# An attention and mixture-of-experts kernel: the row of maxima leaves SyncE's queue for ScalarE's, and subtractions, transposes and gathers change their places in the order

## The chip, the cores and the metric

The kernel runs on one core of a Trainium2 chip. The metric is the device time of one execution in microseconds (us). Five engines work on their own instruction streams, each strictly in order: TensorE (PE, whose weight loads are listed as PEld), VectorE (DVE), ScalarE (ACT), GpSimd (POOL) and SyncE (SP), which here only issues transfers. An engine whose next instruction waits for a semaphore holds up everything behind it on that engine.

## The reference, cut to what matters

Four batches of eight heads, 576 positions, head size 64; then 2304 tokens of width 512 go to one of eight experts each (512 to 1024 to 512).

```python
q_rot, k_rot = rotate(q), rotate(k)                  # rotary embedding
scores = q_rot @ k_rot.T / sqrt(64)
scores -= max(scores, -1)
attn = exp(scores); attn /= attn.sum(-1) + 1e-9
x = (attn @ v) as [2304, 512]
logits = normalised(x) @ normalised(expert_emb).T / tau
expert_idx, gate_w = argmax(logits), its softmax weight
for e in range(8):
    out[mask_e] = gate_w * (relu(x[mask_e] @ w1[e]) @ w2[e])
```

## The kernel before

The work is cut into 16 pairs of heads (four pairs a batch) and then 22 slots of 128 tokens, each slot for one expert. Numbers are carried as a high and a low float16 part where precision needs it, so that many tiles exist twice (`qhi`, `qlo`, `khi`, `klo`, `xh`).

A pair's life: SP loads q and k (576 KB each); POOL rotates them (`rope` steps 0 to 2: two products and a sum for q, the same for k); ACT casts the high parts (step 3), POOL and DVE subtract to get the low parts (step 4: `qlo` on POOL, `klo` on DVE); SP copies them into the operand tiles `QAB`, `KA` and `KB` (`place`). TensorE then computes the scores once with queries as rows (`maxmm`), DVE reduces each block to its row maxima (`maxred`), and TensorE and ACT turn the ten columns of maxima into one row `mr` (`maxend`). That row is copied by a small DMA (2.5 KB, line 189) into row 64 of `QB`, the second half of `QAB`. The scores proper (`smm`, nine steps a pair) multiply `KA` by the queries (line 211) and add the product of `KB` with `QB` (line 215), whose 65th row subtracts the maxima; so line 215 of a pair can't start before its `mr` has landed. ACT takes the exponential (`sexp`, line 226), DVE splits some of it (`ssub`, line 235), TensorE multiplies by the values (`pvw`, `pv`) and DVE normalises into `X` (`pvend`, lines 279 to 283). `R.split` makes the two float16 parts of X: ACT casts the high part (line 450), POOL subtracts for the low part (line 452); every second pair SP transposes them for the router (`turn`) and writes them to memory (`write_x`).

The order on every engine is written by the program: each piece of work is put at a time on a planner's axis (nine units a pair; pair i starts its scores at 9 i), all are sorted by that time and emitted. The numbers of `TIMES` set these times. They are places in an order, not durations. PSUM for the two kinds of scores is a ring of three buffers shared by `maxmm` and `smm`.

After the attention come the slots. A slot gathers its tokens' rows by an indirect DMA that POOL issues (`gather`), SP transposes them by DMA (`xT`), TensorE runs the two layers (`ffn1`, `ffn2`), ACT and DVE split the hidden values, and POOL issues the scattering DMA of the result (`yout`). Each expert's weights come as eight pieces of 512 KB (`load`, into eight single buffers `raw`) where the slot's expert is a new one, and ACT and DVE split them in every slot (`conv`). The first four slots belong to the expert that is most frequent in the first three batches, so that they can start before the last batch is routed (`early`); the last batch's routing (`logits`, `finish`, `late`) runs beside them.

Of the kernel before, what the change touches and what calls it, by code (L numbers as in the profile page):

```python
# [7 lines left out]
F32 = mybir.dt.float32  # L8
F16 = mybir.dt.float16
# [8 lines left out]
B, H, S, D = 4, 8, 576, 64  # L18
NPAIR = 16
# [17 lines left out]
SY = SX * SW * SW  # L37

ORDER = ((0, 0, 0), (1, 0, 0), (0, 0, 1), (1, 0, 1), (0, 1, 0), (1, 1, 0))
TIMES = {"pe1": 1.06, "pvlead": 7.5, "mend": 10.5, "fin": 3, "w": 0.3, "pbufs": 13, "vat": -1, "med": 0.3, "sst": 1.6, "mct": 0.25, "pvt": 0.3, "pe0": 0.9, "d": 0.6, "rdt": 0.9, "e": 0.5, "c0": 126.4, "fin2": 5, "sq": 0.8, "max0": [[-21, 0.5], [0, 0.62], [6.2, 0.85]], "start": [-30, -13, -4, 2.6], "le": 105, "mmt": 0.2, "mlead": 14, "klo": 1, "me0": [-13.5, 6.6], "mdir": 1, "v0": 3, "pl": [[0, 0, 0, 3.3], [0, 1.0, 0.02, 0.1]], "setup": [-59.5, -25, -16.3, 0.7, -59.4, -12.5], "l3": -12, "rk": 23, "ls": 52, "dt": 0.6, "t0": 148.5, "ta": 0.25, "wlead": 10, "cut1": 126, "glead": 20, "s": 0.6, "fin3": -0.45, "r01": [[-30.0, -29.1, -28.2, -27.3, -24.6, -26.4, -25.5, -23.7, -22.8, -16.4], [-25, -24.9, -24.8, -15.5, -14, -24.7, -24.6, -24.5, -13.1, -13.0]], "bw": 2, "cp": [0, 2, 4, 6], "c0d": 4, "lg1": 0.5, "free": [[0.8, 1.4, 1], [2.0, 3.5, 1], [5.7, 6.2, 0]], "fgap": 1.2, "xd": [[0.3, 0.7, 2.8, 2.9], [0.3, 0.7, 2.0, 2.1]], "xd3": [0.02, 0.05, 0.3, 0.31], "xl": 13, "xg": 3, "xl0": 5, "lgd": [12, 12], "tail0": 15}  # L40


def attention(tc, ctx0, ctx, ctx2, ins, xs, R, at, bank, cfg):
    nc = tc.nc
# [14 lines left out]
    QAB, QA, KA, QB, KB = [], [], [], [], []  # L59
# [25 lines left out]
    st = {}  # L85
# [93 lines left out]
    def maxend(i, k):  # L179
        n = i % NB  # L180
        if k == 0:
            ps = bank("mt", 0)
            st["mt", i] = ps
            nc.tensor.transpose(ps[0:10, 0:128], st[i]["m9"], R.ident)
        else:
            ps = st.pop(("mt", i))
            mr = tp.tile([10, 128], F16, tag="mr", name=f"mr_{i}")
            nc.scalar.activation(out=mr, in_=ps[0:10, 0:128], func=AF.Identity, bias=shiftt[0:10], scale=-1.0)  # L188
            (nc.scalar if i == 0 else nc.sync).dma_start(out=QB[n][64:65, 0:1280], in_=mr)

    woven, late = [], []

# [100 lines left out]
    start = cfg["start"]  # L293
    O = cfg.get("o", {})
# [4 lines left out]
    for i in range(NPAIR):  # L299
        g0 = 9 * i  # L300
        r0 = start[i] if i < len(start) else g0 - L - RL
        rdt = cfg.get("rdt", .85)
# [10 lines left out]
        for k, (nm, step) in enumerate((("q", 0), ("q", 1), ("q", 2), ("q", 3), ("k", 0), ("k", 1), ("q", 4), ("k", 2), ("k", 3), ("k", 4))):  # L313
            y = r0 + (k + (step == 4 and nm == "k")) * rdt
            if i < 2:
                y = cfg["r01"][i][5 * (nm == "k") + step]
            if i == 2 and nm == "q" and step == 3:
                y = .2
            if i > 1:
                y += O.get(f"R{nm}{step}", 0)  # L320
            at(y, rope, i, nm, step)
            if step >= 3:
                z = y
                if i < 2:
                    z += cfg.get("pl", ((0, 0, 0, 0), (5, 5, 5, 5)))[i][2 * (nm == "k") + step - 3]
                else:
                    z += O.get(f"D{nm}{step}", 0)
                at(z, place, i, nm, ("hi", "lo")[step - 3])
            if step == 4 and i + 2 < NPAIR:
                at((y + .01 if nm == "q" else -13.06) if i < 1 else cfg.get("l3", -8) if i == 1 else max(-.9, y + .01), load, i + 2, nm)  # L330
# [3 lines left out]
        for s in range(9):  # L334
            ev(f"S{s}", g0 + s, smm, i, s)
            ev(f"E{s}", g0 + s + .1, sexp, i, s)
            ev(f"U{s}", g0 + s + cfg.get("sst", 1.05), ssub, i, s)
            mev(f"M{s}", m0 + md * s + cfg.get("mmt", .2), maxmm, i, s)
            mev(f"C{s}", m0 + md * s + cfg.get("mct", .25), maxred, i, s)
            ev(f"W{s}", g0 + PVL + s + cfg.get("pvt", .3) - .81, pvw, i, s)  # L340
            ev(f"P{s}", g0 + PVL + s + cfg.get("pvt", .3), pv, i, s)
            if s in (4, 8):
                ev(f"X{s // 5}", g0 + PVL + s + cfg.get("pe0", 1.04), pvend, i, s // 5, 0)
                ev(f"Y{s // 5}", g0 + PVL + s + cfg.get("pe1", 1.06), pvend, i, s // 5, 1)
                y = g0 + PVL + s + cfg.get("pe1", 1.06)
                d = cfg["xd"][s // 5] if i < NPAIR - 1 else cfg["xd3"]
                for k in range(2):
                    at(y + d[k], R.split, i, s // 5, k)
                if i % 2:
                    at(y + d[2], R.turn, i, s // 5)  # L350
                    at(y + d[3], R.write_x, i, s // 5)
# [8 lines left out]
class Routing:  # L360
# [93 lines left out]
    def turn(self, i, g):  # L454
        b, kb = i // 4, i % 4 // 2
        if g == 0:
            self.XT[b, kb] = self.xp.tile([128, 9, 2, 128], F16, tag="xt", name=f"xt_{b}_{kb}", bufs=3)
        c = slice(0, 5) if g == 0 else slice(5, 9)
        self.nc.sync.dma_start_transpose(out=self.XT[b, kb][:, c].rearrange("p s t c -> p (s t) c"), in_=self.XH[b, kb][:, c].rearrange("p s t c -> p (s t c)"))

# [237 lines left out]
def moe(tc, ctx, ins, out, xs, R, raw, cfg):  # L698
# [4 lines left out]
    P = {}  # L703

    def open1():
        P["w1"] = pool(name="wring1", bufs=5, side="right")

    def open2():
        P["m"] = pool(name="mtmp", bufs=2, side="right")
# [102 lines left out]
def build(tc, ins, out, cfg=None):  # L812
    cfg = {**TIMES, **(cfg or {})}
    nc = tc.nc
    with ExitStack() as ctx:
# [15 lines left out]
        if True:  # L831
# [40 lines left out]
            for b in range(B):  # L872
# [152 lines left out]
```

## Time and profile before

| | us |
|---|---|
| median of three runs | 632.31 (632.26 to 640.57) |
| the profiled execution | 629.74 |
| its span, first to last instruction | 628.0 |
| TensorE busy | 517.4 (82%) |
| VectorE busy | 473.7 (75%) |
| ScalarE busy | 344.6 (55%) |
| GpSimd busy | 273.0 (43%) |

The shares are means over stages with different limits: the start to about 66 us, eleven pairs to about 259 us, the last pairs with the first routing work to about 358 us, the passage to the experts to about 405 us, and the experts' slots to the end. The profile's page also lists who waited for whom, and where the kernel's time went is read from there stage by stage.

### The profile page before, as it was taken

The page shows a single profiled execution, that of the slowest core. Times are in us where ns is not written, and L with a number is a line of the kernel's source. Part 1 is how long each engine was busy: PE and PEld are TensorE (multiplying, and loading weights), DVE is VectorE, ACT ScalarE, POOL GpSimd, SP SyncE. Part 2 cuts the span into 40 slices and gives each one's busy share as a digit, 9 for nine tenths or more (in the row PEclk, how much of TensorE's full clock was granted, in tenths as well). Part 3 has the DMA queues.
Part 4 walks back from the last instruction along what each step waited for, and adds up shares of the span by engine and source line. Part 5 has one row for each costly group of instructions (what it writes and reads, how often), then busy time and mean ns, then how long its engine had stood idle before and what let it go on. Part 6 is the DMA issues. An engine that isn't in the chain of part 4 may idle for free. (4 is left out here: it accounts for less than half of the span.)

```text
span 628.0 us, 15414 instructions
## 1 busy us (share of the span) xinstructions
PE 517.4 (82%) x5894; PEld 411.2 (65%) x5894; DVE 473.7 (75%) x708; ACT 344.6 (55%) x556; POOL 273.0 (43%) x207
## 2 busy tenths in 40 slices
PE   2488877967897789777688769999899999799994
PEld 1157766856776668666577767868577776586761
DVE  5678877668776775898668516569899999879981
ACT  2244444543433643443445633269789897779862
POOL 6995585648566855774112504213122221411201
PEclk9999789877977896897979978999999999889997
DMA  7875557376295473651762262168934569943210
GB/s 234 227 197 165 154 113 178 92 185 180 69 181 154 104 180 102 149 131 32 176 250 60 60 116 55 44 173 263 300 79 100 152 190 331 294 134 85 70 35 26
DMA packets 87809, 91.35 MB, mean 145 GB/s; under 512 B 50726, under 2 KB 72614, under 8 KB 87728
## 3 DMA queue, kind: packets, MB, share of 16 engines
q1 hardware_dynamic: 83708, 79.27, 49.0%
q0 software_dynamic: 3520, 10.58, 5.7%
q8 instruction: 48, 0.79, 0.5%
q10 hardware_dynamic: 500, 0.45, 0.3%
q14 instruction: 33, 0.27, 0.1%
HBM read 110.60 MB, written 10.56 MB: 193 GB/s over the span
## 5 line engine op out<-in xcount | busy, mean ns | idle before, releaser
L735 DVE SCALAR_TENSOR_TENSOR w<-raw,w 128x1024 f16<-128x1024 f32 x148 | 173.4, 1221 | 18.4 <-ACT w L734 18.4
L226 ACT ACTIVATE p<-st 128x576 f32<-128x576 f32 x144 | 92.3, 646 | 127.3 <-PE st L215 127.1
L175 DVE TENSOR_REDUCE m<-mx 128x1 f32<-128x576 f32 x144 | 107.2, 752 | 66.8 <-PE mx L167 64.8
L245 PEld LDWEIGHTS pv<-V,p 128*128 128x128 f32 (+1 forms) x800 | 118.4, 204 | 54.6 <-issue 51.4
L734 ACT ACTIVATE w<-raw 128x1024 f16<-128x1024 f32 x148 | 146.6, 1047 | 8.2 <-DMA raw<-w 8.2
L761 PE MATMUL h<-xTm,w 128*128 128x128 f16 x2112 | 127.4, 224 | 13.7 <-DMA xTm<-xg 12.9
L761 PEld LDWEIGHTS <-w 128*128 128x128 f16 x2112 | 124.8, 100 | 19.2 <-issue 7.6
L245 PE MATMUL pv<-V,p 128*128 128x65 f32 (+1 forms) x800 | 122.4, 268 | 1.2 <-ACT mr L188 1.2
L215 PE MATMUL st<-QAB,KB 65*128 65x288 f16 x320 | 86.1, 320 | 41.5 <-DMA QAB<-mr 41.5
L782 PE MATMUL yp<-w,hT 128*128 128x512 f16 x528 | 117.5, 379 | 0.0
L787 POOL DMA_INDIRECT out<-y,sidx x22 | 29.1, 1321 | 178.0 <-ACT y L786 168.5
L211 PE MATMUL st<-QAB,KA 128*128 128x288 f16 x320 | 93.3, 313 | 6.0 <-DVE m L175 3.7
L782 PEld LDWEIGHTS <-hT 128*128 128x128 f16 x528 | 50.8, 98 | 57.4 <-issue 0.2
L452 POOL TENSOR_TENSOR xh<-x,xh 128x320 f16<-128x320 f32 (+1 forms) x30 | 26.9, 896 | 121.5 <-ACT xh L450 113.4
L167 PE MATMUL mx<-KA,QAB 128*128 128x288 f16 x300 | 68.6, 325 | 13.3 <-DVE m L175 5.6
L235 DVE TENSOR_TENSOR p<-p 128x576 f16<-128x576 f32 x64 | 70.0, 1093 | 0.7 <-ACT p L226 0.7
L268 PE MATMUL pv<-V,p 128*128 128x65 f16 (+1 forms) x400 | 53.8, 200 | 0.6 <-DVE p L235 0.6
L266 PE MATMUL pv<-V,p 128*128 128x65 f16 (+1 forms) x400 | 54.3, 203 | 0.0
L267 PE MATMUL pv<-V,p 128*128 128x64 f16 (+1 forms) x400 | 54.2, 203 | 0.0
L772 DVE SCALAR_TENSOR_TENSOR hT<-h,hT 128x512 f16<-128x512 f32 x44 | 30.2, 686 | 26.8 <-ACT hT L767 26.8
L167 PEld LDWEIGHTS <-QAB 128*128 128x128 f16 x300 | 32.6, 110 | 25.1 <-issue 15.3
L215 PEld LDWEIGHTS <-KB 65*128 65x128 f16 x320 | 43.8, 145 | 6.5 <-POOL k L122 2.8
(159 smaller groups left out, 676.4 us busy)
## 6 DMA issues: line engine op xcount, KB each, us to landing
raw<-w SPq DMA_DIRECT2D x152, 512.0 KB
q<-qk SPq DMA_DIRECT2D x16, 576.0 KB
k<-qk SPq DMA_DIRECT2D x16, 576.0 KB
v<-v SPq DMA_DIRECT2D x16, 320.0 KB
QAB<-qhi SPq DMA_DIRECT2D x32, 144.0 KB
KA<-khi SPq DMA_DIRECT2D x58, 72.0 KB
xs<-xh SPq DMA_DIRECT2D x16, 256.0 KB
QAB<-qlo SPq DMA_DIRECT2D x32, 72.0 KB
```

What stands on the lines that cost most here:

```text
L167: nc.tensor.matmul(ps[:, c, :288], lhsT=QA[n][:, cols(s, h)], rhs=KA[n][:, H0[h] + c * 288:H0[h] + c * 288 + 288], start=(h == hs[0]), sto ...
L175: nc.vector.tensor_reduce(out=m[:, c:c + 1], in_=st.pop(("mx", i, s))[:, :, :288], op=ALU.max, axis=AX.XY)
L211: nc.tensor.matmul(ps[:, c, :288], lhsT=KA[n][:, cols(s, h)], rhs=QA[n][:, H0[h] + c * 288:H0[h] + c * 288 + 288], start=(h == hs[0]), sto ...
L215: nc.tensor.matmul(ps[:, c, :288], lhsT=KB[n][0:65, cols(s, h)], rhs=QB[n][0:65, H0[h] + c * 288:H0[h] + c * 288 + 288], start=False, stop ...
L226: nc.scalar.activation(out=p.rearrange("p (c x) -> p c x", c=2), in_=st.pop(("s", i, s))[:, :, :288], func=AF.Exp, scale=0.125)
L235: nc.vector.tensor_tensor(out=lo, in0=p, in1=hi, op=ALU.subtract)
L245: nc.tensor.matmul(o, lhsT=lt, rhs=rt, start=first, stop=False, skip_group_check=True)
L266: nc.tensor.matmul(o[:, 0:65], lhsT=ph, rhs=vv[:, 0:65], start=False, stop=False, skip_group_check=True)
L734: nc.scalar.activation(out=d[:, 0], in_=raw[c], func=AF.Copy, scale=SW)
L735: nc.vector.scalar_tensor_tensor(out=d[:, 1], in0=raw[c], scalar=SW, in1=d[:, 0], op0=ALU.mult, op1=ALU.subtract)
L761: nc.tensor.matmul(ps[:, f], lhsT=wd[:, wi, jj * 512 + f * 128:jj * 512 + f * 128 + 128], rhs=xt[:, 4 * jj + 2 * jp + xi], start=(jp == 0 ...
L782: nc.tensor.matmul(ps, lhsT=ht[:, hi, 2 * c + ii], rhs=wd[:, wi, ii * 512:(ii + 1) * 512], start=(c == 0 and k == 0), stop=(c == 3 and k = ...
```

## The change

Four things change; the amount of work does not. First, the small DMA of `mr` is issued by ACT for every pair (before: for pair 0 alone, SP for the rest). Second, for pairs 0 to 10 POOL's subtraction of the first half of X stands behind the rotations that it stood in the middle of, and SP's transposes and writes of X move behind the placing of the next k parts; SP also issues a pair's `qlo` behind the next load of q. Third, the gathered rows and their transposes get a pool of their own that opens at an earlier switch (`open1`), so that the gathers of the first four slots stand earlier on POOL, and SP's transposes of every slot stand further ahead in SP's queue (`xl` 13 to 20; `glead` moves too). Fourth, the router's transposed X has two buffers in place of three, and the last batch's logits stand later on TensorE (`tail0` 15 to 18).

```diff
-TIMES = {... "glead": 20, ... "xd": [[0.3, 0.7, 2.8, 2.9], [0.3, 0.7, 2.0, 2.1]], ... "xl": 13, ... "xl0": 5, ... "tail0": 15}
+TIMES = {... "glead": 30, ... "xd": [[0.4, 3.9, 5.9, 5.91], [0.3, 0.9, 3.0, 3.01]], "xd2": [0.2, 0.5, 2.0, 2.01], "xi": 11, "pd": [0.3, 1.2, 0.3, 0.3], ... "gx": 12, "xl": 20, ... "xl0": 10, ... "tail0": 18}
...
-            (nc.scalar if i == 0 else nc.sync).dma_start(out=QB[n][64:65, 0:1280], in_=mr)
+            nc.scalar.dma_start(out=QB[n][64:65, 0:1280], in_=mr)
...
-                    z += O.get(f"D{nm}{step}", 0)
+                    z += cfg["pd"][2 * (nm == "k") + step - 3]
...
-                d = cfg["xd"][s // 5] if i < NPAIR - 1 else cfg["xd3"]
+                d = cfg["xd"][s // 5] if i < cfg["xi"] else cfg["xd2"] if i < NPAIR - 1 else cfg["xd3"]
...
-            self.XT[b, kb] = self.xp.tile([128, 9, 2, 128], F16, tag="xt", name=f"xt_{b}_{kb}", bufs=3)
+            self.XT[b, kb] = self.xp.tile([128, 9, 2, 128], F16, tag="xt", name=f"xt_{b}_{kb}", bufs=2)
...
     def open1():
         P["w1"] = pool(name="wring1", bufs=5, side="right")
+        P["x"] = pool(name="xgath", bufs=4, side="right")
...
-        xg = P["m"].tile([128, PITCH], F32, tag="xg", name=f"xg_{t}", bufs=4)
+        xg = P["x"].tile([128, PITCH], F32, tag="xg", name=f"xg_{t}")
...
-        d = st["xT", t] = P["m"].tile([128, 8, 128], F16, tag="xT", name=f"xTm_{t}", bufs=3)
+        d = st["xT", t] = P["x"].tile([128, 8, 128], F16, tag="xT", name=f"xTm_{t}", bufs=3)
...
                     e1 = plan(t, gen, "c" * 5 + ".b" + "d" * 4)
+                    end11 = end
...
-                sc.at(max(T0 + DT * (G - cfg.get("glead", 22)), ready) if t >= NE else max(cut2 + .05, e1) + t * .01, M["gather"], t)
+                sc.at(max(T0 + DT * (G - cfg.get("glead", 22)), ready) if t >= NE else max(end11 + cfg["gx"], e1) + t * .01, M["gather"], t)
```

ACT's stream in a pair of the steady part, after the change (`p` are the exponentials of the steps, `mr` the row of maxima of the next pair, `khi` and `xh` casts):

```order
L226 ACTIVATE p_5_678<-st_5_671 128x576
L188 ACTIVATE mr_700<-mt_688,shiftt 10x128
L189 DMA QAB_135<-mr_700 1x10x128
L226 ACTIVATE p_6_710<-st_6_703 128x576
L226 ACTIVATE p_7_737<-st_7_729 128x576
L125 CAST khi_742<-k_421 128x576
```

The DMA of line 189 is the row that is new on ACT; before, these rows stood there without it and the row stood on SP, as the next piece shows.

SP's queue in such a pair before (`QAB<-qhi`, `QAB<-qlo`, `KA<-khi`, `KB<-klo` place the parts of a later pair; `q` and `k` are loads of 576 KB):

```order
L139 DMA QAB_135<-qhi_1122 64x2x576 x2
L141 DMA QAB_135<-qlo_1219 64x576 x2
L90 DMA q_1223<-qk 128x1152
L189 DMA QAB_129<-mr_1237 1x10x128
L144 DMA KA_136<-khi_1277 64x576
```

and after:

```order
L139 DMA QAB_135<-qhi_1122 64x2x576 x2
L90 DMA q_1220<-qk 128x1152
L141 DMA QAB_135<-qlo_1218 64x576 x2
L144 DMA KA_136<-khi_1276 64x576
L145 DMA KA_136<-khi_1276 64x576
```

The row of maxima no longer stands behind the placing of `qlo`, which POOL's subtraction has to release.

POOL's stream in such a pair before (line 452 makes the low part of X, lines 118 to 122 rotate, line 130 subtracts for `qlo`):

```order
L118 TENSOR_TENSOR k_423<-k_423,cost 128x576
L452 TENSOR_TENSOR xh_0_636<-x_620,xh_0_636 128x5x64
L120 TENSOR_TENSOR k_423<-k_423,sint 128x576
L130 TENSOR_TENSOR qlo_685<-q_346,qhi_583 128x576
L122 TENSOR_TENSOR k_423<-k_423 128x576
L452 TENSOR_TENSOR xh_0_636<-x_620,xh_0_636 128x4x64
```

and after:

```order
L118 TENSOR_TENSOR k_421<-k_421,cost 128x576
L120 TENSOR_TENSOR k_421<-k_421,sint 128x576
L130 TENSOR_TENSOR qlo_684<-q_344,qhi_581 128x576
L122 TENSOR_TENSOR k_421<-k_421 128x576
L452 TENSOR_TENSOR xh_0_636<-x_620,xh_0_636 128x5x64
L452 TENSOR_TENSOR xh_0_636<-x_620,xh_0_636 128x4x64
```

Both subtractions of X now follow the last sum of the rotations. On POOL at the passage to the experts, after the change (`w_2`, `w_4` are parts of weights; `xg` the first gathers; `xh_1` belongs to pair 14):

```order
L733 TENSOR_TENSOR w_2_4530<-ws_4531,w_2_4530 128x1024
L745 DMA xg_4653<-xs,gidx 128x520
L745 DMA xg_4655<-xs,gidx 128x520
L745 DMA xg_4657<-xs,gidx 128x520
L745 DMA xg_4659<-xs,gidx 128x520
L452 TENSOR_TENSOR xh_1_4668<-x_4053,xh_1_4668 128x5x64
L452 TENSOR_TENSOR xh_1_4668<-x_4053,xh_1_4668 128x4x64
```

Before, the two subtractions of pair 14 stood ahead of the four gathers.

## Rows read from the trace of the kernel before

**Rows 1.** Waits view: waiting group, releaser, us in total, times, longest.

```profile
PE st L215 <- DMA QAB<-mr: 41.5, 13, 5.0
```

**Rows 2.** Timeline of PE: start, us, instruction, idle time before it and its releaser.

```profile
68.02 0.40 PE L215 MATMUL st<-QAB,KB 65*128 65x288 f16 x1 [1.90 <-DMA QAB<-mr]
...
89.20 0.40 PE L215 MATMUL st<-QAB,KB 65*128 65x288 f16 x1 [4.09 <-DMA QAB<-mr]
...
109.80 0.40 PE L215 MATMUL st<-QAB,KB 65*128 65x288 f16 x1 [3.85 <-DMA QAB<-mr]
...
259.02 0.38 PE L215 MATMUL st<-QAB,KB 65*128 65x288 f16 x1 [3.95 <-DMA QAB<-mr]
```

**Rows 3.** Timelines of ACT, POOL and SP, 99 to 107 us.

```profile
100.85 0.34 ACT L188 ACTIVATE mr<-mt,shiftt 10x128 f16<-10x128 f32 x1
...
99.44 0.79 POOL L452 TENSOR_TENSOR xh<-x,xh 128x320 f16<-128x320 f32 x1 [6.05 <-ACT xh L450]
...
102.11 1.83 POOL L130 TENSOR_TENSOR qlo<-q,qhi 128x576 f16<-128x576 f32 x1
...
103.97 1.13 SPq L141 DMA_DIRECT2D QAB<-qlo  x2
...
105.83 0.81 SPq L189 DMA_DIRECT2D QAB<-mr  x1
```

**Rows 4.** Windows: us, busy of PE, PEld, DVE, ACT, POOL, clock, DMA share, GB/s.

```profile
85.10:89.20 4.10, 0.01 (x2) 0.00 (x1) 3.64 (x5) 1.64 (x5) 3.65 (x3) 0.90 0.95 210
89.20:95.30 6.10, 6.10 (x39) 4.71 (x39) 2.38 (x4) 1.85 (x4) 4.12 (x3) 0.51 0.72 183
95.30:105.90 10.60, 10.60 (x150) 9.72 (x150) 8.59 (x15) 5.07 (x10) 5.87 (x4) 1.00 0.78 152
...
48.10:66.10 18.00, 15.71 (x197) 13.70 (x196) 16.34 (x25) 8.60 (x16) 9.23 (x7) 1.00 0.56 163
```

**Rows 5.** Windows by stage.

```profile
66.10:259.00 192.90, 154.97 (x1755) 134.15 (x1754) 141.83 (x216) 85.01 (x182) 124.94 (x85) 0.82 0.58 140
...
358.00:405.00 47.00, 37.69 (x507) 31.73 (x508) 19.47 (x62) 16.65 (x37) 10.33 (x8) 0.89 0.40 82
405.00:628.00 223.00, 206.14 (x2270) 148.50 (x2266) 189.74 (x186) 172.49 (x202) 48.34 (x38) 0.97 0.57 158
```

**Rows 6.** Timelines of ACT and PE at pair 0.

```profile
20.04 1.52 ACTq L189 DMA_DIRECT2D QAB<-mr  x1
...
22.47 0.64 PE L215 MATMUL st<-QAB,KB 65*128 65x288 f16 x2 [2.37 <-DMA QAB<-mr]
```

**Rows 7.** Lines 235 and 122 by source: count, ns min/median/max, first and last start.

```profile
L235 DVE TENSOR_TENSOR p<-p x64: 794/1052/2010, 38.8 to 355.0; 128x576 f16<-128x576 f32 x64
...
L122 POOL TENSOR_TENSOR k<-k x15: 1391/1400/1949, 19.7 to 297.4; 128x576 f32<-128x576 f32 x15
```

**Rows 8.** Timelines of POOL, SP and PE at the passage to the experts.

```profile
345.62 2.14 POOL L732 TENSOR_TENSOR w<-ws,w 128x1024 f16<-128x1024 f32 x1 [2.64 <-ACT w L731]
...
355.22 1.58 POOL L744 DMA_INDIRECT xg<-xs,gidx  x1 [0.29 <-issue]
...
359.32 1.23 SPq L749 DMA_TRANSPOSE xTm<-xg  x1
...
364.11 2.74 PE L761 MATMUL h<-xTm,w 128*128 128x128 f16 x24 [6.18 <-DMA xTm<-xg]
```

**Rows 9.** Timeline of PE: the last batch's logits.

```profile
377.75 0.18 PE L489 MATMUL lg<-emb,xt 128*128 128x16 f16 x1 [3.20 <-DMA xt<-xh]
```

**Rows 10.** Timelines of PE and ACT in the experts' slots.

```profile
447.40 5.52 PE L761 MATMUL h<-xTm,w 128*128 128x128 f16 x96 [2.55 <-DMA xTm<-xg]
...
547.52 7.93 PE L761 MATMUL h<-xTm,w 128*128 128x128 f16 x96 [4.14 <-DMA xTm<-xg]
...
549.04 1.06 ACT L734 ACTIVATE w<-raw 128x1024 f16<-128x1024 f32 x1 [2.90 <-DMA raw<-w]
```

**Rows 11.** Timeline of SP: the placing of the low part of k.

```profile
93.20 1.10 SPq L147 DMA_DIRECT2D KB<-klo  x2
```

More of the change, by code (lines that the diff above doesn't have):

```diff
@@ L39 @@
 ORDER = ((0, 0, 0), (1, 0, 0), (0, 0, 1), (1, 0, 1), (0, 1, 0), (1, 1, 0))
-TIMES = {"pe1": 1.06, "pvlead": 7.5, "mend": 10.5, "fin": 3, "w": 0.3, "pbufs": 13, "vat": -1, "med": 0.3, "sst": 1.6, "mct": 0.25, "pvt": 0.3, "pe0": 0.9, "d": 0.6, "rdt": 0.9, "e": 0.5, "c0": 126.4, "fin2": 5, "sq": 0.8, "max0": [[-21, 0.5], [0, 0.62], [6.2, 0.85]], "start": [-30, -13, -4, 2.6], "le": 105, "mmt": 0.2, "mlead": 14, "klo": 1, "me0": [-13.5, 6.6], "mdir": 1, "v0": 3, "pl": [[0, 0, 0, 3.3], [0, 1.0, 0.02, 0.1]], "setup": [-59.5, -25, -16.3, 0.7, -59.4, -12.5], "l3": -12, "rk": 23, "ls": 52, "dt": 0.6, "t0": 148.5, "ta": 0.25, "wlead": 10, "cut1": 126, "glead": 20, "s": 0.6, "fin3": -0.45, "r01": [[-30.0, -29.1, -28.2, -27.3, -24.6, -26.4, -25.5, -23.7, -22.8, -16.4], [-25, -24.9, -24.8, -15.5, -14, -24.7, -24.6, -24.5, -13.1, -13.0]], "bw": 2, "cp": [0, 2, 4, 6], "c0d": 4, "lg1": 0.5, "free": [[0.8, 1.4, 1], [2.0, 3.5, 1], [5.7, 6.2, 0]], "fgap": 1.2, "xd": [[0.3, 0.7, 2.8, 2.9], [0.3, 0.7, 2.0, 2.1]], "xd3": [0.02, 0.05, 0.3, 0.31], "xl": 13, "xg": 3, "xl0": 5, "lgd": [12, 12], "tail0": 15}
+TIMES = {"pe1": 1.06, "pvlead": 7.5, "mend": 10.5, "fin": 3, "w": 0.3, "pbufs": 13, "vat": -1, "med": 0.3, "sst": 1.6, "mct": 0.25, "pvt": 0.3, "pe0": 0.9, "d": 0.6, "rdt": 0.9, "e": 0.5, "c0": 126.4, "fin2": 5, "sq": 0.8, "max0": [[-21, 0.5], [0, 0.62], [6.2, 0.85]], "start": [-30, -13, -4, 2.6], "le": 105, "mmt": 0.2, "mlead": 14, "klo": 1, "me0": [-13.5, 6.6], "mdir": 1, "v0": 3, "pl": [[0, 0, 0, 3.3], [0, 1.0, 0.02, 0.1]], "setup": [-59.5, -25, -16.3, 0.7, -59.4, -12.5], "l3": -12, "rk": 23, "ls": 52, "dt": 0.6, "t0": 148.5, "ta": 0.25, "wlead": 10, "cut1": 126, "glead": 30, "s": 0.6, "fin3": -0.45, "r01": [[-30.0, -29.1, -28.2, -27.3, -24.6, -26.4, -25.5, -23.7, -22.8, -16.4], [-25, -24.9, -24.8, -15.5, -14, -24.7, -24.6, -24.5, -13.1, -13.0]], "bw": 2, "cp": [0, 2, 4, 6], "c0d": 4, "lg1": 0.5, "free": [[0.8, 1.4, 1], [2.0, 3.5, 1], [5.7, 6.2, 0]], "fgap": 1.2, "xd": [[0.4, 3.9, 5.9, 5.91], [0.3, 0.9, 3.0, 3.01]], "xd2": [0.2, 0.5, 2.0, 2.01], "xi": 11, "pd": [0.3, 1.2, 0.3, 0.3], "xd3": [0.02, 0.05, 0.3, 0.31], "gx": 12, "xl": 20, "xg": 3, "xl0": 10, "lgd": [12, 12], "tail0": 18}
 def attention(tc, ctx0, ctx, ctx2, ins, xs, R, at, bank, cfg):
```

## The prediction

> **What bounds the kernel now.** I read the waits view first, for TensorE, since it is busy most. Its largest wait is that of line 215 for the DMA of `mr`: 41.5 us in 13 waits [rows 1]. The timeline places them: one at the first step of each pair from pair 2 to pair 11, ten in all, the first before 68.02 us, the last before 259.02 us, most of them close to 4 us [rows 2]; the others are the 2.37 us of pair 0 and small ones near the end, which I leave out.
>
> Why `mr` comes late is read from ACT, POOL and SP beside each other [rows 3]. ACT has the row ready at 100.85 + 0.34 = 101.19. SP issues its DMA only at 105.83, because `qlo` stands ahead of it in SP's queue and waits for POOL's subtraction, which runs from 102.11 to 103.94. POOL is late because its subtraction of X waited 6.05 us for ACT's cast and holds the rotations behind it. From issue to TensorE's start is 109.80 - 105.83 = 3.97 us. So of the 8.6 us between the row and its use, 4.64 pass before anything is sent.
>
> What a pair costs without the wait: the stretch around the wait before 89.20 shows TensorE idle for 4.10 us, then busy without a gap for 6.10 us at a granted clock of 0.51 and for 10.60 us at 1.00 [rows 4]. 0.51 is the lower of its two levels, 1.2 GHz, and it comes right behind the idle 4 us. At 2.4 GHz the 6.10 us would be about 3.1, and TensorE's own work in a pair 13.7. VectorE did 3.64 us of its work in the idle stretch, so it has 3.64 + 2.38 + 8.59 = 14.6 us in this pair, and 141.83 / 9 = 15.8 on the mean of the nine pairs [rows 4, 5]. VectorE is therefore next.
>
> **The change part by part.** *The row of maxima on ACT.* It removes the wait for `qlo` from the path. ACT's own DMA of pair 0 took from 20.04 to 22.47, 2.43 us, until TensorE started [rows 6]; SP's took 3.97. From 101.19 that lands at 103.6 or at 105.2; line 215 wants it at 109.80 - 3.85 = 105.95. Both are in time, so I take the wait as gone. The issue occupies ACT for 0.8 us (SP's row) to 1.5 us (ACT's own) a pair; ACT is busy 85.01 of 192.90 us [rows 3, 5, 6] and waits mostly for TensorE's scores, so I price it at nothing; without that cover it is 9 x 1.5 = 14 us.
>
> *What is late next.* With the wait gone a pair can't be shorter than VectorE's 15.8 us. A pair that had no such wait and ran at a granted clock of 1.00 is in the trace: pair 1, where VectorE was busy 16.34 of 18.00 us and idle 1.66 [rows 4] (more reductions fall there than in a later pair). 15.8 of work and 1.0 to 1.7 of idle time make 16.8 to 17.5; the gapless part of a pair with half its clock lost is 6.10 + 10.60 = 16.7. I take 17.0. The stretch from 66.10 to 259.00 holds the first wait and nine pairs, 192.9 us [rows 5]; nine pairs of 17.0 are 153, a gain of 40. Bounds: 15.8 a pair (VectorE never idle) gives 192.9 - 142 = 51; 18.3, worked out below as a rival, gives 28.
>
> *POOL's subtractions behind the rotations.* `qlo`, `khi` and the loads of q and k come earlier by the 6 us that POOL waited; they are two to three pairs ahead of their use, so this earns nothing itself, but it keeps POOL off the path: POOL's 124.94 / 9 = 13.9 us a pair [rows 5] fit in 17.0 as one block. The low part of X and its transposes come later by some units; the router reads them more than a pair later in batches 0 and 1, which hides it. If that cover were gone, one transpose's landing, some 5 us (359.32 to 364.11 [rows 8]), would show twice. SP's new order (`qlo` behind a load, transposes behind `klo`) costs nothing for the same lead. The transposed X with two buffers: by the planned times the logits that read the older tile stand ahead of the transpose that overwrites it, so nothing waits.
>
> *The last pairs.* From 259 to 358 us only one short wait for `mr` is left, and routing work on VectorE and a late transpose hold TensorE; none of that is touched. I take 1 us, between 0 and 4.
>
> *The first gathers.* They were issued from 355.22 on, behind the subtractions of pair 14; now they follow the weights' subtraction that ends at 345.62 + 2.14 = 347.76 [rows 8]. Gather to transpose took 359.32 - 355.22 = 4.1 us and transpose to TensorE 364.11 - 359.32 = 4.8, so the rows land at about 347.8 + 8.9 = 356.7, and TensorE, idle from 364.11 - 6.18 = 357.9, finds them. That returns 6.18 us. The 24 matmuls behind the wait took 2.74 us; the same 24 by the pace of the slots, 5.52 for 96 [rows 10], take 1.4, so another 1.3 us come back, of which with the following matmuls I take 1.5. The logits of the last batch now stand behind one more such block of 24, which fills 1.3 of the 3.20 us that they wait [rows 9]. Sum 9; bounds 3 (the gathers wait for the lists and half is lost) and 11 (both waits whole). The cost, pair 14's subtractions some 2 to 3 us later, falls on tiles that are transposed with pair 15.
>
> *Transposes further ahead.* In SP's queue a slot's transpose now stands ahead of four weight loads. The two large waits of the slots are for such transposes: 2.55 and 4.14 us, and the second is followed by 96 matmuls in 7.93 us in place of 5.52 [rows 10], 9.1 in all. The loads that it overtakes come later, and ACT already waits 2.90 us for one beside the second wait [rows 10]. I take 6 of 9.1; bounds 0 and 9.1. The other slots have no gap to close.
>
> **The sum.** 40 + 1 + 9 + 6 = 56 us. From the profiled execution's 629.74 that is 573.7; it lies 2.6 below the median of 632.31, so I add 2.6: 576. The bounds of the terms together are 28 + 0 + 3 + 0 = 31 and 51 + 4 + 11 + 9 = 75: 601 and 557.
>
> **The rivals.** *GpSimd and VectorE in each other's way.* The same subtraction of line 235 takes 794 to 2010 ns and the same sum on POOL 1391 to 1949 [rows 7]: the two slow each other when they meet, and in shorter pairs they meet more often. If they excluded each other, POOL's 13.9 us and VectorE's four subtractions at 0.79 with some 1.2 us for its other two of the kind would make 18.3 us a pair. That is a gain of 28 in place of 40: 588. For it: POOL now works in one block; against it: part of POOL's 13.9 is already such waiting. The Trainium skill, "SBUF — State Buffer", section "Who interferes with whom", says that a VectorE operation with two inputs in SBUF and a GpSimd operation that reads SBUF exclude each other, the later one waiting in full; the spread of both rows agrees with it. Chance 0.16.
>
> *The row still lands late.* More transfers are in flight beside it, and if it took twice SP's price, 7.9 us, it would land at 109.1 and 3.2 us of each wait would stay: 9 x 3.2 = 29 less, 605. Against it: most of its delay was before the issue. The Trainium skill, "DMA: Bandwidth & Descriptors", section "Issuing engines are not separate DMA queues", says that another issuing engine only saves the sequencer's time, the transfers sharing the same 16 DMA engines; taken alone that would leave a gain of SP's 0.81 us a pair, and no row here shows more than the queue's part of it. Chance 0.06.
>
> *VectorE was the bound all along.* The 3.64 us that it works in the idle stretch would be paid elsewhere, and a pair would shrink by only 4.10 - 3.64 = 0.5: 4 + 16 = 20 in all, 612, or no measurable change if the later terms fail too. Against it: in the rest of the pair VectorE is idle 16.70 - 10.97 = 5.7 us [rows 4]. Chance 0.09.
>
> *Slower: ACT held by its own DMA.* By its semaphores, ACT's DMA waits for the transfer eight places earlier, in every second pair the placing of `klo`, which SP issues. Everything behind it on ACT, the exponentials above all, waits too. Now `klo` goes out at 93.20 [rows 11], 8.0 us before the row is ready at 101.19, and if it lands 4 us later, as the row does now, the slack is 4.0. If SP fell 12 us behind, ACT would stand 8.0 us in a pair; nine pairs of 17.0 + 8.0 are 225, 32 more than now, and with the 16 gained elsewhere the time is 648. It makes the kernel slower from (192.9 + 16) / 9 - 17.0 = 6.2 us a pair on. Against it: SP has lost its long wait for the row and POOL comes earlier. Chance 0.04.
>
> **How the numbers follow.** The forecast (557 to 601, likeliest 576) has 0.65, the rivals 0.16, 0.06, 0.09 and 0.04. The range from 561 to 602 leaves out the outer twentieths of the forecast and the last three rivals, about 0.2. 2 per cent, 12.6 us, is about what a measurement of this kernel can tell from no change: faster 0.91 (forecast, first two rivals, under half of the third), same 0.05, slower 0.04.
>
> **What would show it.** In the changed kernel's profile: no waits of line 215 for `mr` above 1 us between 66 and 230 us; POOL's long waits for ACT's cast behind the rotations and not in them; a granted clock near 1.00 in the pairs in place of 0.82; a distance of about 17 us from pair to pair, with VectorE over 90% busy; TensorE going from the last `pv` into the first slot without 6 us of idle; no wait above 1 us for `xTm`. The prediction is wrong if the pairs keep 20 us with another releaser in line 215's place, or if the exponentials wait on ACT behind its DMA.

## The result, and the profile after

The changed kernel takes 590.52 us (median; 586.74 to 595.88), the kernel before 632.5 beside it; the ratio is 0.931, with a 95% interval from 0.9235 to 0.939. Measured once more beside later runs it took 590.56 us, with a ratio of 0.947 (0.942 to 0.952). The forecast was 576, in the range from 561 to 602: the side is right, the gain is 14 us smaller than forecast.

The stages are cut at one mark that all kernels have, VectorE's copy of a pair's maxima (line 177), and at the first matmul of the experts' slots. The rows of the changed kernel below are from its execution with a span of 590.8 us.

| us | before | changed | gain | forecast |
|---|---|---|---|---|
| start to the maxima of pair 3 | 66.19 | 66.16 | 0.0 | 0 |
| nine pairs, maxima of 3 to 12 | 190.35 | 167.30 | 23.1 | 40 |
| maxima of pair 12 to 15 | 68.65 | 66.42 | 2.2 | 1 |
| to the first matmul of the slots | 38.92 | 36.86 | 2.1 | 9 and 6 together |
| slots to the end | 263.89 | 254.06 | 9.8 | (see above) |
| span | 628.0 | 590.8 | 37.2 | 56 |

The table compares two executions, and the gain of the medians is 34 to 42 us. The marks cut the tenth wait for the row, the one before 259.02 [rows 2], so that most of it stands in the third line. In the window for which the 40 was worked out, from 66.10 to 259.00, the attention took 192.9 us; in the changed kernel, from the first line 215 of pair 2 (65.99) to that of pair 11 (232.92), it takes 166.9, a gain of 26, and the rest up to the maxima of pair 15 gains nothing (66.2 before, 67.0 after). One term carries most of the miss: a pair takes 167.30 / 9 = 18.6 us and not 17.0. The waits view of the changed kernel says who holds TensorE now:

```profile
PE mx L167 <- DVE m L175: 19.4, 12, 4.5
...
ACT qhi L125 <- POOL q L122: 19.1, 11, 4.4
...
PE st L211 <- DVE m L175: 13.6, 10, 3.9
...
PE st L215 <- DMA QAB<-mr: 2.8, 2, 1.9
...
PE h L762 <- DMA xTm<-xg: 0.6, 1, 0.6
```

The row of maxima, 41.5 us before [rows 1], is down to 2.8; the transposes that the slots waited for, 2.55, 4.14 and 6.18 [rows 8, 10], to 0.6. In their place stand 33 us for `m`, VectorE's row maxima, in lines 167 and 211; in the kernel before these two were 9.3:

```profile
PE mx L167 <- DVE m L175: 5.6, 2, 4.9
...
PE st L211 <- DVE m L175: 3.7, 4, 1.9
```

The windows view of the nine pairs, and of one pair in them (us, busy of PE, PEld, DVE, ACT, POOL, clock, DMA share, GB/s), answers to [rows 4, 5]:

```profile
66.16:233.46 167.30, 143.13 (x1758) 125.09 (x1758) 142.87 (x210) 84.10 (x182) 118.68 (x85) 0.92 0.65 159
...
158.56:176.67 18.11, 15.92 (x189) 13.86 (x188) 14.93 (x22) 8.65 (x17) 12.62 (x10) 0.91 0.82 172
```

VectorE does 142.87 / 9 = 15.9 us a pair, as forecast; but it is idle for 2.7 us a pair, and the granted clock is 0.92 and not 1.00. Where the idle time comes from is seen in the timelines of POOL, VectorE, TensorE and ACT at a pair's start, with the row of maxima on ACT, which answers to [rows 3], as the last group:

```profile
176.22 0.67 POOL L452 TENSOR_TENSOR xh<-x,xh 128x256 f16<-128x256 f32 x1 [5.42 <-ACT xh L450]
176.84 1.96 POOL L118 TENSOR_TENSOR q<-q,cost 128x576 f32<-128x576 f32 x1
178.77 1.65 POOL L120 TENSOR_TENSOR q<-q,sint 128x576 f32<-128x576 f32 x1
180.50 1.79 POOL L122 TENSOR_TENSOR q<-q 128x576 f32<-128x576 f32 x1
...
176.74 0.84 DVE L235 TENSOR_TENSOR p<-p 128x576 f16<-128x576 f32 x1
177.48 1.69 DVE L110 SCALAR_TENSOR_TENSOR V<-v,V 128x320 f16<-128x320 f32 x1
179.08 1.95 DVE L130 TENSOR_TENSOR klo<-k,khi 128x576 f16<-128x576 f32 x1
180.96 0.74 DVE L175 TENSOR_REDUCE m<-mx 128x1 f32<-128x576 f32 x1
...
181.75 0.43 PE L167 MATMUL mx<-KA,QAB 128*128 128x288 f16 x2 [1.75 <-DVE m L175]
...
171.51 0.34 ACT L188 ACTIVATE mr<-mt,shiftt 10x128 f16<-10x128 f32 x1
171.89 0.72 ACTq L189 DMA_DIRECT2D QAB<-mr  x1
```

Three operations of VectorE with two inputs (the splits of `p` and `V`, the subtraction for `klo`) stand in a row ahead of the reduction that TensorE waits for, and GpSimd begins its next rotation just beside them, since it has waited 5.42 us for ACT's cast of X until then. `V` takes 1.69 us and `klo` 1.95. The pair that ends a batch is worse: all three are long (1.90, 1.69 and 1.95 from 120.65 on), and TensorE waits 3.92 us. That this is what the missing gain went into is an inference from one profile, which the experiments put to the test.

### The profile page after: what moved, and what is told of

Read it like the earlier page. It is cut to its first block, busy times and chain, and to the rows that moved or that the text cites. A ratio compares the mean times of both kernels' runs of the same rounds, so it can differ in the third digit from the quotient of the medians.

```text
span 594.1 us, 15336 instructions
## 1 busy us (share of the span) xinstructions
PE 508.6 (86%) x5894; PEld 401.8 (68%) x5894; DVE 478.8 (81%) x708; ACT 342.5 (58%) x556; POOL 320.4 (54%) x207
## 5 line engine op out<-in xcount | busy, mean ns | idle before, releaser
L736 DVE SCALAR_TENSOR_TENSOR w<-raw,w 128x1024 f16<-128x1024 f32 x148 | 173.4, 1223 | 16.1 <-ACT w L735 13.6
L735 ACT ACTIVATE w<-raw 128x1024 f16<-128x1024 f32 x148 | 148.0, 1052 | 16.7 <-DMA raw<-w 16.4
L788 POOL DMA_INDIRECT out<-y,sidx x22 | 70.9, 3224 | 117.0 <-ACT y L787 98.2
L245 PEld LDWEIGHTS pv<-V,p 128*128 128x128 f32 (+1 forms) x800 | 116.2, 202 | 15.7 <-issue 10.9
L762 PEld LDWEIGHTS <-w 128*128 128x128 f16 x2112 | 119.6, 98 | 7.7 <-issue 2.7
L762 PE MATMUL h<-xTm,w 128*128 128x128 f16 x2112 | 122.6, 219 | 2.1 <-DMA xTm<-xg 2.1
L245 PE MATMUL pv<-V,p 128*128 128x65 f32 (+1 forms) x800 | 120.8, 267 | 1.1 <-ACT mr L188 1.1
L167 PE MATMUL mx<-KA,QAB 128*128 128x288 f16 x300 | 63.6, 305 | 29.1 <-DVE m L175 21.7
L215 PE MATMUL st<-QAB,KB 65*128 65x288 f16 x320 | 82.5, 310 | 2.9 <-DMA QAB<-mr 2.9
L452 POOL TENSOR_TENSOR xh<-x,xh 128x320 f16<-128x320 f32 (+1 forms) x30 | 25.2, 840 | 104.4 <-ACT xh L450 96.3
L167 PEld LDWEIGHTS <-QAB 128*128 128x128 f16 x300 | 30.7, 103 | 42.0 <-issue 34.0
L211 PEld LDWEIGHTS <-KA 128*128 128x128 f16 x320 | 40.0, 126 | 14.6 <-issue 11.9
```

Source lines behind the costliest of these rows:

```text
L167: nc.tensor.matmul(ps[:, c, :288], lhsT=QA[n][:, cols(s, h)], rhs=KA[n][:, H0[h] + c * 288:H0[h] + c * 288 + 288], start=(h == hs[0]), sto ...
L211: nc.tensor.matmul(ps[:, c, :288], lhsT=KA[n][:, cols(s, h)], rhs=QA[n][:, H0[h] + c * 288:H0[h] + c * 288 + 288], start=(h == hs[0]), sto ...
L215: nc.tensor.matmul(ps[:, c, :288], lhsT=KB[n][0:65, cols(s, h)], rhs=QB[n][0:65, H0[h] + c * 288:H0[h] + c * 288 + 288], start=False, stop ...
L245: nc.tensor.matmul(o, lhsT=lt, rhs=rt, start=first, stop=False, skip_group_check=True)
L735: nc.scalar.activation(out=d[:, 0], in_=raw[c], func=AF.Copy, scale=SW)
L736: nc.vector.scalar_tensor_tensor(out=d[:, 1], in0=raw[c], scalar=SW, in1=d[:, 0], op0=ALU.mult, op1=ALU.subtract)
```

## The experiments

**The parts of the change.** Four kernels take it apart. The first is the kernel before with the row of maxima on ScalarE:

```diff
-            (nc.scalar if i == 0 else nc.sync).dma_start(out=QB[n][64:65, 0:1280], in_=mr)
+            nc.scalar.dma_start(out=QB[n][64:65, 0:1280], in_=mr)
```

> The kernel before with one edit: ScalarE issues the row of maxima of every pair; GpSimd's order and the late part stay as before. Theory A (the queue ahead of the row is the whole wait, and behind it a pair is bound by VectorE with GpSimd in its way): the waits of line 215 for the row go, and nearly all that the attention stage gained in the changed kernel (about 24 us) comes with this edit, 605 to 612 us. Rival B (GpSimd's rotations, still held 6 us in each pair by its subtraction of X, become late for the next pair): the row's wait is replaced by one for the placed parts of q and k, and over 620 us are left.

Measured: 604.11 us, ratio 0.967 (0.958 to 0.976), 23 us less than the kernel before beside it, 1 us under the bounds of theory A; rival B is refuted. Nine pairs take 164.4 us, 18.3 a pair, and TensorE's timeline shows the new wait in place of the row's:

```profile
89.54 0.41 PE L167 MATMUL mx<-KA,QAB 128*128 128x288 f16 x2 [1.74 <-DVE m L175]
...
106.96 0.41 PE L167 MATMUL mx<-KA,QAB 128*128 128x288 f16 x2 [1.71 <-DVE m L175]
...
128.16 0.41 PE L211 MATMUL st<-QAB,KA 128*128 128x288 f16 x2 [3.84 <-DVE m L175]
```

The second run is the changed kernel with that line as before (the reverse of the diff above):

> The changed kernel with one edit taken back: SyncE issues the row of maxima again, behind qlo, for all pairs but pair 0. Theory A (the row was late only by what stood ahead of it in SyncE's queue): with GpSimd's subtraction for qlo no longer held up, SyncE reaches the row near the time at which it is ready, and it lands about 4 us after; some waits of 0 to 2 us come back, 592 to 602 us. Rival B (only the move to ScalarE helps, the order on GpSimd nothing): waits of 3 to 4 us for the row in ten pairs come back, 610 to 618 us.

Measured: 591.06 us, ratio 0.941 (0.932 to 0.950), the changed kernel's time. SyncE's timeline tells why, and corrects the words of the expectation: in the new order the row no longer stands behind `qlo` but ahead of it.

```profile
97.95 0.54 SPq L90 DMA_DIRECT2D q<-qk  x1
98.59 0.81 SPq L189 DMA_DIRECT2D QAB<-mr  x1
99.44 1.18 SPq L141 DMA_DIRECT2D QAB<-qlo  x2
```

The row, ready at 95.76, goes out at 98.59 and costs TensorE 1.63 us at 102.33; in all 6.0 us of waits for it are left, in 5, and rival B's are not there. The third run, the kernel before with the attention's parts alone (the row, and the numbers `xd`, `xd2`, `xi` and `pd` with the two lines that read them):

> The kernel before with the attention's part of the change alone (row on ScalarE, GpSimd's subtractions of X behind its rotations, SyncE's order); gathers and x^T as before. Theory A: the attention stage is as in the changed kernel, some 24 us shorter, the passage to the experts as before: 604 to 610 us. Against the row alone the order on GpSimd earns under 4 us. Rival B: the order on GpSimd is what the pairs needed, and this kernel is 10 us or more ahead of the row alone.

Measured: 606.71 us, 0.966 (0.958 to 0.973): the same as the row alone within the uncertainty, so that rival B is refuted. Either edit frees the row, the order as the second run shows it, and the second of the two adds nothing. The fourth run has the late part alone:

```diff
+        P["x"] = pool(name="xgath", bufs=4, side="right")
...
-"glead": 20, "xl": 13, "xl0": 5, "tail0": 15
+"glead": 30, "xl": 20, "xl0": 10, "tail0": 18, "gx": 12
```

> The kernel before with the late part alone: the pool of their own for the gathered rows, gathers ahead of pair 14's subtractions, x^T and gathers further ahead, two buffers for the router's transposed X. Theory A (as predicted: 9 for the first gathers and 6 for the transposes further ahead, both apart from the attention): 614 to 620 us. Rival B (the late gain is only had when the attention ends early): within 5 us of the kernel before, 627 to 632 us.

Measured: 615.13 us, 0.978 (0.970 to 0.986), 12.2 us less, as theory A has it. The first matmul of the slots comes at 359.21 without a wait (364.11 before [rows 8]), and the slots last 255.2 us in place of 263.9. The attention's part (20.6) and the late part make 32.8, the row alone (23.2) and the late part 35.4; the second run, which equals the changed kernel, gained 36.2 beside the same executions of the kernel before, and the whole change 34 to 42. Within the uncertainty the two halves add up.

**Why a pair takes 18.6 us.** The changed kernel was profiled again beside three variants of it.

> The changed kernel once more, for a second profile of it beside the kernels below. Both theories: 585 to 592 us; pairs without routing work 17.2 us apart, TensorE waiting 1.75 us for a row-maximum of VectorE in each, and 3.8 us in the pairs that end a batch.

Measured: 590.56 us; its rows are those of the section above. The waits are as expected; the plain pairs stand 17.9 to 18.2 us apart, up to 1 us more than expected, at a clock of 0.90 to 0.91. The next kernel has no rotations:

```diff
+        if i > 1 and step < 3:
+            return
```

> The changed kernel without GpSimd's rotations (two products and a sum for q and for k) from pair 2 on; q and k go unrotated into the scores, everything else is there. Theory S (VectorE's operations with two inputs are stretched while GpSimd works: the split of p 0.83 to 1.83, of V 0.50 to 1.70, of klo 0.74 to 1.95 us, and this delays the row-maxima that TensorE waits for at the start of each pair): these three stand at their short durations, the waits for m at a pair's start fall under 1 us, the pairs come to 15 to 16 us, and thirteen pairs gain 2 to 3 us each: 550 to 562 us. Rival T (VectorE's own work and the order of its reductions hold TensorE, GpSimd has no part in it): the pairs stay at 17 us or more, 582 to 592 us.

Measured: 614.55 us in all, which says nothing here, since other scores send other tokens to the experts and the slots alone last 333 us. The nine pairs are what was asked for (windows view from the maxima of pair 3 to those of pair 12, and VectorE's timeline at a pair's start; the line numbers are two higher from line 118 on):

```profile
62.71:195.02 132.31, 128.57 (x1758) 114.91 (x1757) 110.83 (x211) 83.09 (x182) 28.45 (x30) 1.00 0.86 201
```

```profile
150.28 0.84 DVE L237 TENSOR_TENSOR p<-p 128x576 f16<-128x576 f32 x1
151.01 0.48 DVE L110 SCALAR_TENSOR_TENSOR V<-v,V 128x320 f16<-128x320 f32 x1
151.41 0.75 DVE L132 TENSOR_TENSOR klo<-k,khi 128x576 f16<-128x576 f32 x1
```

132.31 / 9 = 14.7 us a pair, with TensorE busy for 14.3 of them at a clock of 1.00. In the same order, `V` and `klo` are at 0.48 and 0.75 us, and no wait of TensorE for `m` above 1 us is left in these pairs. T is refuted, S holds for the pairs. One thing is not separated by this run: ACT, too, no longer waits for GpSimd's rotated q (19.1 us in the changed kernel).

The next kernel moves four squares on ScalarE:

```diff
-... else end + .02 + (cfg.get("sq", .6) if b < B - 1 else .05) * (k - 5), R.square, b, k)
+... else end + (2.22 if b < B - 1 else .02) + (cfg.get("sq", .6) if b < B - 1 else .05) * (k - 5), R.square, b, k)
```

> The changed kernel with one edit: four of the nine squares that ScalarE takes at the end of a batch (batches 0 to 2) stand some two units later, behind the start of the next pair. Rival A (the exponentials behind ScalarE's squares delay TensorE and with it VectorE there, so that the two waits of 3.85 us in the pairs that end a batch are ScalarE's): these waits fall to the 1.75 us of the other pairs and the half clock behind them goes, 3 to 4 us each: 578 to 584 us. Theory S (the waits are VectorE's three stretched operations, ScalarE has no part): the waits stay above 3 us, 585 to 592 us.

Measured: 591.2 us, 0.951 (0.945 to 0.957), no change. The waits fall from 3.92 and 3.90 to 3.39 each: half a microsecond is the squares', the rest is not.

```profile
125.66 0.41 PE L211 MATMUL st<-QAB,KA 128*128 128x288 f16 x2 [3.39 <-DVE m L175]
...
200.13 0.64 PE L211 MATMUL st<-QAB,KA 128*128 128x288 f16 x2 [3.39 <-DVE m L175]
```

The last of the four moves `klo` and the split of V into the time in which GpSimd waits:

```diff
-        ev("VH", y, vhi, i)
-        ev("VL", y + 1, vlo, i)
+        at(y - (i > 1), vhi, i)
+        at(y + 1 - 1.3 * (i > 1), vlo, i)
+TIMES = {... "o": {"Rk4": -1.4}, ...}
```

The number `Rk4` moves `klo`, and with it SyncE's placing of `klo` and its next load of k, by the same 1.4 units; what that part brings was not tried by itself.

> The changed kernel with one edit: from pair 2 on VectorE's subtraction for klo and its split of V stand behind the last normalisation of X of the pair before, where GpSimd waits for ScalarE's cast of X (3.9 to 5.9 us in each pair), and ScalarE's casts of V one unit earlier; the work is the same. Theory S: both run there at about 0.74 and 0.50 us in place of 1.95 and 1.70, the row-maxima at the pair's start come 3 to 4 us earlier, the waits of 1.75 us go, VectorE's work in a pair falls from 15.8 to about 13.5 us: pairs of 15.5 to 16.5 us, 568 to 580 us. Rival T (the durations don't hang on GpSimd): both stay long, stand in front of the last row-maximum of a pair and delay it; 588 to 600 us.

Measured: 564.59 us, 0.905 (0.900 to 0.910): 26 us faster than the changed kernel, 3 us under theory S's bounds, and the fastest here but for the variant with the row on SyncE below, which is its equal. VectorE's and POOL's timelines, and the windows view of the nine pairs:

```profile
177.03 0.42 DVE L283 TENSOR_TENSOR x<-pv,pvr 128x256 f32<-128x256 f32 x1
177.37 0.75 DVE L130 TENSOR_TENSOR klo<-k,khi 128x576 f16<-128x576 f32 x1
178.04 0.49 DVE L110 SCALAR_TENSOR_TENSOR V<-v,V 128x320 f16<-128x320 f32 x1
178.46 0.76 DVE L175 TENSOR_REDUCE m<-mx 128x1 f32<-128x576 f32 x1
...
179.32 1.84 DVE L235 TENSOR_TENSOR p<-p 128x576 f16<-128x576 f32 x1
...
178.43 0.67 POOL L452 TENSOR_TENSOR xh<-x,xh 128x256 f16<-128x256 f32 x1 [3.00 <-ACT xh L450]
179.06 1.41 POOL L118 TENSOR_TENSOR q<-q,cost 128x576 f32<-128x576 f32 x1
```

```profile
67.44:215.47 148.03, 132.08 (x1764) 116.25 (x1764) 137.12 (x210) 84.95 (x181) 123.37 (x86) 1.00 0.74 184
```

The pairs come to 148.03 / 9 = 16.4 us, plain ones to 15.4 to 15.9, at a clock of 1.00. But the way is not quite what was expected: VectorE's work falls only from 15.9 to 15.2 us a pair, not to 13.5. Over the whole kernel `V` falls from 23.0 to 15.6 us and `klo` from 27.2 to 12.9, 21.7 together, and the splits of `p`, which now meet the rotations, take 12.8 of it back (66.7 to 79.5 us). By this account 0.6 of the 2.1 us a pair is work, and the larger part is place: the stretched operations no longer stand in a row ahead of a reduction that TensorE waits for, VectorE's idle time falls from 2.7 to 1.2 us a pair, and the clock stays up.

**What hangs on what.** Four more kernels. The kernel before with this last diff alone:

> The kernel before, with the edit to VectorE's order alone (klo and the split of V behind the last normalisation of X of the pair before, from pair 2 on); the row of maxima stays on SyncE behind qlo. Theory S (two bounds stand in a row: first the row, then VectorE): the pairs are still held by the row, which VectorE's earlier work doesn't bring sooner, so that the waits of 3.5 to 5 us for it stay: within 6 us of the kernel before, 618 to 628 us. Rival U (VectorE's stretched operations also delay the row itself, by the reductions): the pairs shrink by 2 us or more, 600 to 610 us.

Measured: 628.76 us beside 628.6, ratio 1.005 (1.001 to 1.009). VectorE works less there (131.53 us in the 190.00 from 66 to 256, 138.97 in the kernel before), and nothing comes of it, since the row's waits stay:

```profile
PE st L215 <- DMA QAB<-mr: 41.1, 12, 5.2
```

The faster kernel with the row's DMA on SyncE again:

> The changed kernel with klo and V earlier (as in the run of that name) and SyncE issuing the row of maxima again. With pairs of 17 to 18 us the row came in time from SyncE too. Theory A (the row has then about 1 us of slack, and shorter pairs use it up): with pairs near 16 us it is late by 1 to 3 us in each, 572 to 588 us. Rival B (in shorter pairs qlo comes earlier too, so that the row keeps its slack): 562 to 569 us, as with the row on ScalarE.

Measured: 564.25 us, 0.903 (0.894 to 0.911): rival B. The row's waits are 6.7 us in 6, the longest 1.9, and pairs are 16.0 us. Theory A's slack of 1 us was wrong; the work ahead of the row comes earlier with the shorter pairs. In the two profiles the nine pairs are 144.3 us with the row on SyncE and 148.0 with it on ScalarE, so that in short pairs ScalarE's issue may not be free; the medians, 564.25 and 564.59, don't show it. The faster kernel with GpSimd's and SyncE's order of before:

```diff
-"xd": [[0.4, 3.9, 5.9, 5.91], [0.3, 0.9, 3.0, 3.01]], "xi": 11, "pd": [0.3, 1.2, 0.3, 0.3]
+"xd": [[0.3, 0.7, 2.8, 2.9], [0.3, 0.7, 2.0, 2.1]], "xi": 15, "pd": [0, 0, 0, 0]
```

> The changed kernel with klo and V earlier, and GpSimd's and SyncE's order of the attention as in the kernel before (subtractions of X in the middle of the rotations). The work and its order on VectorE are those of the run with klo and V earlier; GpSimd's idle time lies elsewhere. Theory S (what counts is that klo and V meet an idle GpSimd): one or both are stretched again in most pairs, 570 to 582 us. Rival V (what counts is only that they stand ahead of the last row-maximum, not in front of the next pair's): 562 to 568 us.

Measured: 573.48 us, 0.916 (0.906 to 0.927). The time is in theory S's bounds, but not for its reason: `klo` and `V` have the same medians as in the faster kernel (0.76 and 0.97 us), and plain pairs are 15.8 to 16.1. Of the 7.2 us between the two spans, 5.2 lie in the nine pairs, most of it in two pairs behind a batch's end, 18.7 and 21.6 us in place of 16.9 and 19.8, with waits of line 167 for ACT's exponentials (1.28 us at 148.96) that the faster kernel doesn't have there; another 5.2 lie between the maxima of pair 15 and the slots, and the rest gives 3 back. The second 5.2 can't be put down to the order: it is the same work at a clock of 0.86 in place of 1.00, and the changed kernel, which has the new order, ran that stretch at 0.86 too. So the new order on GpSimd and SyncE, worth nothing while `klo` and `V` hold the pair, is worth 9 us by the medians once they don't, of which the profiles place 5 in the pairs; which of its steps it is was not tried. Last, `klo` moved alone:

> The changed kernel with klo alone moved forward behind the last normalisation of X; the split of V stays at the pair's start. Theory S: klo falls from 1.95 to 0.75 us and leaves the front of the first row-maximum, V stays long; some two thirds of the gain of both, 570 to 576 us. Rival W (the gain hangs on both being away, since V then only moves into klo's place and one wait of the kind stays): under a third of it, 582 to 590 us.

Measured: 582.56 us, 0.928 (0.919 to 0.938), a third of the gain of both: rival W. VectorE's timeline shows where `klo`'s 1.2 us went:

```profile
171.20 0.75 DVE L130 TENSOR_TENSOR klo<-k,khi 128x576 f16<-128x576 f32 x1
171.86 0.75 DVE L175 TENSOR_REDUCE m<-mx 128x1 f32<-128x576 f32 x1
...
172.72 1.80 DVE L235 TENSOR_TENSOR p<-p 128x576 f16<-128x576 f32 x1
174.41 1.68 DVE L110 SCALAR_TENSOR_TENSOR V<-v,V 128x320 f16<-128x320 f32 x1
176.00 0.74 DVE L175 TENSOR_REDUCE m<-mx 128x1 f32<-128x576 f32 x1
```

The split of `p` ahead of `V`, 0.84 us in the changed kernel, now meets the rotation and takes 1.80; a wait of 2.0 to 2.1 us for the reduction behind them stays in seven of the nine pairs.

## Why the prediction was right and where it was wrong

*The wait for the row.* Right, with its cause. The wait was made in SyncE's queue, behind a DMA that waited for GpSimd, and not by the row's own transfer: the row alone on ScalarE takes it away, and so, but for 6.0 us, does the order that puts it ahead of `qlo` on SyncE. The issue on ScalarE takes 0.72 us, under the 0.8 to 1.5 of the prediction, and is hidden as taken in pairs of 18.6 us. The rivals of a late row and of ScalarE held by its DMA didn't come about. On the page cited for the late row: the Trainium skill, "DMA: Bandwidth & Descriptors", section "Issuing engines are not separate DMA queues", says that another issuing engine saves only the sequencer's time. By that rule, the run with the row back on SyncE agrees (591.06 beside 590.52 us); the 23 us of the row alone on ScalarE are more than that: they are the wait that stood ahead of the row in SyncE's stream.

*What is late next.* This is the step that failed: "15.8 of work and 1.0 to 1.7 of idle time make 16.8 to 17.5 ... I take 17.0". The work came out as 15.9 us, though the 15.8 had been read over a window longer than nine pairs: between the marks it was 15.5 in the kernel before, and the stretch of `V` grew (16.0 to 23.0 us over the kernel). The idle time was mis-sized, 2.7 in place of 1.0 to 1.7, so that the term brought 26 us and not 40, under its lower bound of 28. Of the signs that the prediction named, the waits for the row and for `xTm` went as said, but the clock in the pairs is 0.92 and not near 1.00, and VectorE is busy for 15.9 of 18.6 us, 85% and not over 90%. The idle time was read from pair 1, one pair, as if idle time were a fixed allowance. It is made by the order: the two engines wait for each other by turns, TensorE for a reduction, VectorE then for the next scores, and how long is set by what stands ahead of that reduction on VectorE. The three operations there could be read from the order and from [rows 7], which show how far one of them stretches; they stood in a row at a pair's start already in the kernel before, beside the wait for the row:

```profile
66.26 1.99 DVE L235 TENSOR_TENSOR p<-p 128x576 f16<-128x576 f32 x1
68.15 1.68 DVE L110 SCALAR_TENSOR_TENSOR V<-v,V 128x320 f16<-128x320 f32 x1
69.75 1.96 DVE L130 TENSOR_TENSOR klo<-k,khi 128x576 f16<-128x576 f32 x1
```

Removing GpSimd's rotations gives 14.7 us a pair, and two of the three moved away 16.4.

*GpSimd and VectorE in each other's way.* This rival names what happened, and its 588 us is near, in part by luck: its 18.3 us, the sum of GpSimd's busy time and VectorE's short operations, would be a floor for any order, and the faster kernel, with GpSimd busy 123.37 / 9 = 13.7 us a pair, goes below it by 1.9. The sum took GpSimd's busy time with the stretch in it, as its text says, and counted that twice. With GpSimd's operations at their shortest too (six of 1.39 us, 1.27 for `qlo`, 0.79 and 0.67 for X, 11.1 together) and VectorE's 4.4, the same sum is an estimate of 15.5; the plain pairs of the two fastest kernels, 15.4 to 15.9 and 14.8 to 15.2, lie about there. So the size is refuted, and not that the two keep each other out. The rival of VectorE as the bound all along (612) is refuted in its size: 3.64 us worked in the idle time did not have to be paid in full.

*The order on GpSimd.* Priced at nothing, and it is nothing beside the row on ScalarE (606.71 and 604.11 us). It was wrong to call it without effect on the path in general: it would have freed most of the row's wait on SyncE too, and with `klo` and `V` out of the way it is worth some 5 to 9 us.

*The late part.* Forecast 9 and 6, measured 12.2 alone, and 11.9 in the stages of the whole change: right in mechanism, 3 us under. The waits that were named are gone, and the cover for pair 14's later subtractions held. Two things that the prediction did not have stand against it. TensorE runs the stretch from pair 15 to the slots at a lower clock than before; below stand the kernel before, the changed kernel, and its variant with the later squares, whose work there is the changed kernel's (windows view, columns as in [rows 4]):

```profile
325.19:364.11 38.92, 29.24 (x437) 26.05 (x437) 24.70 (x64) 22.71 (x45) 12.24 (x11) 0.97 0.31 71
...
299.88:336.74 36.86, 33.39 (x437) 29.73 (x437) 26.01 (x63) 20.16 (x34) 11.83 (x11) 0.86 0.30 71
...
301.14:332.88 31.74, 28.69 (x438) 25.73 (x436) 24.63 (x63) 19.72 (x34) 12.28 (x11) 1.00 0.34 81
```

At a clock of 1.00 this stretch is 5 us shorter, more than the 3 that are missing. And TensorE has a wait in the last batch's routing that the kernel before doesn't have:

```profile
355.94 0.17 PE L528 MATMUL rank<-ohall,tri 128*128 128x8 f16 x1 [3.87 <-DVE ohall L520]
```

*The last pairs:* forecast 1, within 0 to 4; measured nothing, since the 2.2 us of the table are the end of the tenth wait for the row.

What stays open is the size of the clock's part. In the run of the attention's part alone, whose attention has the same order, two pairs with the wait of 1.75 us were 17.2 us long at a clock of 1.00; in the changed kernel pairs with that wait were 17.9 to 18.2 at 0.90 to 0.91. It is not the program: the changed kernel's own other profile (span 594.1) has three such pairs of 17.2 at 1.00. No run here tells what decides it.

## What to carry to other kernels

When the largest wait is removed, the next bound is not the busiest engine's work plus a little: look at what stands on that engine ahead of the one instruction that the waiting engine needs, and price those operations at the duration they have there. Two edits that free the same wait don't add up, and an edit behind a bound brings nothing until the bound goes: the same move of `klo` and `V` was worth 0 us on the kernel before and 26 on the changed one. Operations of VectorE with two inputs belong where GpSimd stands idle, and moving one of a group may only hand its stretch to its neighbour.

## What was unexpected of the hardware

The stretch is large, and it spares the reductions: `V` takes 0.48 us without GpSimd's rotations beside it and 1.69 with them, `klo` 0.75 and 1.95, while the row-maxima between them stay at 0.73 to 0.76 us in either case. In the faster kernel `V` has a median of 0.97, when it meets GpSimd's work for a part only. GpSimd's products stretch as well, 1.40 to 1.96 us. The Trainium skill, "SBUF — State Buffer", section "Who interferes with whom", says that the later of two such operations waits in full for the other; in the rows above, `V` starts at 177.48 beside a product that ends at 178.80, and itself ends at 179.17, 0.37 us later, a little under its own short duration of 0.48. The trace agrees with the rule. What it costs hangs on the order: with the same operations a pair took 18.6 or 16.4 us.
